# Gating of five batches: sums and products on GpSimd, spread over more turns, two batches overlapping

## The chip, the core and the metric

The kernel runs on one core of a Trainium2 chip, with TensorE (PE), VectorE (DVE), ScalarE (ACT), GpSimd (POOL) and the sync engine's DMA queue (SP). The metric is device time in microseconds, median of three executions. One more execution was profiled, and every row below comes from it.

## What is computed

Block-causal attention feeds a mixture-of-experts layer in which every token goes to one expert and every expert keeps at most `capacity` tokens. Cut from the reference:

```
scores = scale * q @ k.T                       # 8 batches x 8 heads, 576 x 64, f32
attn   = softmax(where(block_i >= block_j, scores, -1e9))
x      = (attn @ v) as [B*S, H*D]              # 4608 x 512
logits = x @ w_gate                            # 8 experts
expert_idx = argmax(logits);  gate_w = softmax(logits)[expert_idx]
for e: tok = the `capacity` tokens of e with the largest gate_w
       out[tok] = gate_w[tok] * (relu(x[tok] @ w1[e]) @ w2[e])
```

## The kernel before

The order of every engine's instructions is written out by hand. The main loop has 32 **turns**, one for each pair of heads, four pairs to a batch. The list `TURN` names the steps of a turn and to which pair each belongs: loads five pairs ahead (`load`), preparation of q and k two pairs ahead (`prep`), scores, row maxima (`max`, `merge`) and exponentials (`soft`) of the next pair, and transposes back (`back`), copies out of PSUM (`take`) and products with v (`values`) of the present pair.

Some names that the steps need:

- `merge` (line 593) is one small DVE operation in each turn; ACT's next exponentials read its result. Turns are measured here from one merge to the next, and turn i ends at the merge of pair i+1.
- `prep 0` comes right behind `merge` on DVE (`STREAM_TRANSPOSE`, line 529); GpSimd then scales its result (`qt`, line 536), and the step `ends` (line 570) on PE reads that at the next turn's start. Behind the scaling, GpSimd issues the loads of v (line 522), some of the loads of weights (line 332), and two loads of k (line 514).
- `ends`, `scores 2` (PE, lines 570, 553, then the mask, 579), then `back` (634), `scores 1` and `scores 3`, the mask again, then `values` (652). `max 56 0` is the first DVE maximum of a turn and reads `scores 2`.
- SP issues loads of q and k for the pair five ahead, and the stores of a batch's sums and rows (`store`, lines 387 to 393).

**Gating** of a batch is done in the four turns after its last pair. A queue `small` of generators is advanced by the steps `t`, one instruction each: one `t` opens the turn, `pe` follows it, then come five more, and a seventh stands between `scores 3` and `max 08 1`, shortly before `values`. `pe` issues the logits' products on PE in the first of the four turns and their transposes (`logits2`, line 417) in the second, into the PSUM banks that `scores 1` and `back B` also use.

Per batch the queue holds `recip` (six DVE instructions), `store`, `products` (four DVE products with `rs` into `prod`, line 423, and the sum over heads into `lg`, line 427), `shift` (maximum `mx`, line 432, and difference `dl`), then `expo` on ACT (step `ta`), `first_of` (four DVE instructions), `weight` (three), `turn` (one product on GpSimd into `sp`, line 463), `turn2` (16 small PE matmuls at the head of `values`, line 472) and `placed` (one DVE copy, line 478). Before, these fall as follows:

```
first turn   placed of the batch before, recip 1 to 5; recip 6 in the seventh slot;  PE: logits
second turn  store; products (4), sum over heads; mx in the seventh slot;            PE: logits2
third turn   dl, eq, eq * iota, min, eq;  expo
fourth turn  sum, reciprocal, Gm;  GpSimd: sp;                                       PE: turn2
```

The first of the batches has no `placed` ahead of its `recip`, so that in its first turn (turn 5) all six stand in the opening slots, and no `turn2` was in the turn before. Batch b has its four turns at i = 4b+5 to 4b+8.

Of the kernel before, what the change touches and what calls it, by code (L numbers as in the profile page):

```python
# [7 lines left out]
F32 = mybir.dt.float32  # L8
# [5 lines left out]
ALU = mybir.AluOpType  # L14
AX = mybir.AxisListType
# [3 lines left out]
P = 128  # L19
BLK = 64  # L20
NT = 5
# [148 lines left out]
def tile_attn_moe(ctx, tc, q, k, v, w_gate, w1, w2, capacity, out, xs=None, dbg=None):  # L170
    nc = tc.nc
    B, H, S, D = q.shape
    NTOK, DM = out.shape
    E, _, F = w1.shape
# [18 lines left out]
    sm = att2.enter_context(tc.tile_pool(name="sm", bufs=4))  # L193
# [51 lines left out]
    iota_e = sm1.tile([P, E], F32, name="iota_e")  # L245
    iota_v = sm1.tile([P, NT, E], F32, name="iota_v")
    Gm = const.tile([P, NC, E], F32, name="Gm")
    prod = sm1.tile([P, NT, H, E], F32, name="prod")
# [22 lines left out]
    dl = sm1.tile([P, NT, E + 1], F32, name="dl")  # L271
# [47 lines left out]
    def weights(n, after=None):  # L319
        for _ in loads(n, after):  # L320
            pass

    def loads(n, after=None):

        nonlocal nw, loaded
        for _ in range(n):
            src, e = wlist[nw]
            w_ = wpools[nw % len(wpools)].tile([P, KP * F], F32, name="w")
            nw += 1
            wt_[src is w2, e] = w_ = w_.rearrange("p (a f) -> p a f", f=src.shape[2])  # L330
            if nw <= FW0:
                yield from (nc.gpsimd.dma_start(w_[:, a], src[e][a * P:(a + 1) * P]) for a in range(w_.shape[1]))
                continue
            with ExitStack() as order:
                if loaded is not None:
                    order.enter_context(tc.issue_after(loaded.ins))
                load = loaded = nc.sync.dma_start(w_, src[e].rearrange("(a p) f -> p a f", p=P))
            if after is not None:
                tc.add_manual_dep(load.ins, after.name, mybir.DependencyInfo(
                    mybir.DependencyClass.Sync, mybir.DependencyReason.DATA))  # L340
# [14 lines left out]
    def banks(use, where=BANKS):  # L355
        return [psp[i].tile([P, 512], F32, name=f"bank{i}") for i in where[use]]

    class Batch:
# [61 lines left out]
        def products(self):  # L420
            for pr in range(NP):
                iv = self.la[pr // 2][:, 0:BLK * NT].rearrange("p (t r c) -> p t r c", t=NT, r=2)[:, :, pr % 2, 0:2 * E]
                yield nc.vector.tensor_tensor(
                    prod[:, :, 2 * pr:2 * pr + 2], iv.rearrange("p t (s e) -> p t s e", s=2),
                    self.rs[:, :, 2 * pr:2 * pr + 2].unsqueeze(3).broadcast_to([P, NT, 2, E]), op=ALU.mult)
            self.lg = sm.tile([P, NT, E], F32, name="lg", bufs=2)
            yield nc.vector.tensor_reduce(self.lg, prod.rearrange("p t h e -> p t e h"), axis=AX.X, op=ALU.add)

# [20 lines left out]
        def weight(self):  # L449
            vec = nc.vector  # L450
            N = NT
            g = sm.tile([P, N], F32, name="g", bufs=2)
            yield vec.tensor_reduce(g, dl, axis=AX.X, op=ALU.add)
            yield vec.reciprocal(g, g)
            yield vec.tensor_tensor(Gm[:, N * self.b:N * (self.b + 1)], self.eq,
                                    g.unsqueeze(2).broadcast_to([P, N, E]), op=ALU.mult)

        def turn(self, eng, n=1):

            self.sp = sp = sm.tile([P, E, NT, 8], F32, name="sp", bufs=1)  # L460
            G = Gm[:, NT * self.b:NT * (self.b + 1)].rearrange("p t e -> p e t")
            for s_ in range(n):
                eng.tensor_tensor(
                    sp[:, s_:E:n], G[:, s_:E:n].unsqueeze(3).broadcast_to([P, E // n, NT, 8]),
                    sameE.unsqueeze(1).unsqueeze(1).broadcast_to([P, E // n, NT, 8]), op=ALU.mult)
# [21 lines left out]
    HW = NW // 2  # L487

    batches = {}

    class Pair:

# [179 lines left out]
    def warm(n, wt, after=None):  # L672

        if not n:
            return
        with ExitStack() as order:
            if after is not None:
                order.enter_context(tc.issue_after(after.ins))
            for i in range(n):
                nc.tensor.matmul(wt.rearrange("p (a c) -> p a c", c=P), lhsT=identr,  # L680
                                 rhs=identr.unsqueeze(1).broadcast_to([P, 4, P]), start=(i == 0), stop=(i == n - 1))

    n = B * NP
# [7 lines left out]
    wg_v = w_gate.rearrange("(r s d) e -> s d r e", s=2, d=D)  # L691
    cleared, kept = 0, 2

    pe_, small, acts, turns, issued = [], [], [], [], {None}

    def enqueue(bt):

        def mark(tag):
            return lambda: issued.add((bt, tag))

        def fill(f, need=None, then=()):
            small.append((f(), need and (bt, need), then))

        pe_.extend(([bt.logits], [bt.logits2, mark("l2")]))
        fill(bt.recip, None, (bt.store,))
        fill(bt.products, "l2")
        fill(bt.shift, None, (mark("sub"),))
        fill(bt.first_of)
        fill(bt.weight, "ge", (lambda: bt.turn(nc.gpsimd), lambda: turns.append((bt, mark("t2")))))
        fill(bt.placed, "t2")  # L710
        acts.append((bt.expo, (bt, "sub"), mark("ge")))

    def pe():
# [1 line left out]
            f()  # L715

    def t():
        while small:
            g_, need, then = small[0]
            if need not in issued or next(g_, None) is not None:  # L720
                return
            small.pop(0)
            for f in then:
                f()

    def ta():
        if acts and acts[0][1] in issued:
# [10 lines left out]
    with tc.manual_schedule():  # L738
        warm(WARM[0], banks("g")[0])
        early = loads(FW0)  # L740
        for i in range(-LEAD, n):
            if i == -1:
                nc.sync.dma_start(ci, capacity.bitcast(U32).partition_broadcast(P))
                for h in range(2):
                    nc.sync.dma_start(wgd[h * D:(h + 1) * D, :, h * E:(h + 1) * E], wg_v[h])

            for _ in range(min(4, nz - kept - cleared) if i >= n - 5 else 0):
                clear(cleared, nc.sync)
                cleared += 1
            if i == 1 - LEAD:  # L750
                nc.scalar.activation(early_exp, ramp[:, 2, 0:1], AF.Exp)
                constants()
            if i == -1:
                constants2()
            if i == 1:
                constants3()
            if i >= 2 and i % 3:
                next(early, None)
            for d, what, *args in FIRST if i == -1 else AHEAD if i == -2 else TURN if i < n - 1 else LAST:
                if what in slots_:  # L760
                    slots_[what]()
                elif 0 <= i + d < n and not (what == "flip" and n - NP <= i + d < n - 2):
                    getattr(pairs[i + d], what)(*args)
            if n - NP <= i + valued < n - 2:
                pairs[i + valued].flip()
            if i >= flipped and (i - flipped) % NP == NP - 1 and i - flipped < n - 1:
                enqueue(batches[(i - flipped) // NP])
        for _ in early:
            pass
        while not turns:  # L770
            t()
        bt = batches[B - 1]
        pairs[n - 2].flip()
        for _ in bt.recip():
            pass
        bt.store_sums()
        to, from_ = pairs[n - 1].out.pop("V0")
        pairs[n - 1].take("V1", "v")
        nc.scalar.copy(to[:, 0], from_[:, 0])
        nc.vector.tensor_copy(to[:, 1], from_[:, 1])  # L780
        att.close()
        fwa = late.enter_context(tc.tile_pool(name="fwa", bufs=FWA, **right, **tw))
        wpools += [fwa] * FWA
        lt = bt.logits_of()
        pairs[n - 1].flip()
        bt.store_x()
        weights(1)
        bt.logits_out(lt)
        bt.logits2()
        bt_, mark = turns.pop(0)  # L790
        bt_.turn2(banks("av")[0])
        mark()
        for _ in (*bt.products(), *bt.shift()):
            pass
        bt.expo()
        while small:
            t()
        found, weighed = bt.first_of(), bt.weight()
        for g_ in (found, found, found, weighed, found, weighed, weighed):
            next(g_)  # L800
        bt.turn(nc.vector, 2)
        bt.turn2(banks("L")[0])
        for _ in bt.placed():
            pass
# [7 lines left out]
    vec = nc.vector  # L812
    pool = nc.gpsimd
# [323 lines left out]
    with tc.If(again > 0):  # L1137
# [8 lines left out]
        eq = gen.tile([P, CP, E], F32, name="eq")  # L1146
# [15 lines left out]
        step = 1.0  # L1162
# [161 lines left out]
```

## Time and profile before

| | |
|---|---|
| median of 3 executions | 396.84 us (396.63 to 399.62) |
| profiled execution | 397.45 us, span 395.7 us, so 1.75 us lie around the span |
| granted TensorE clock | 0.995 of full speed |
| busy share of the span | PE 95%, DVE 72%, ACT 73%, POOL 43% |

The main loop ends at about 280 us; the experts' layer follows. Busy time of PE is modelled from pipelined matmuls, so that a full PE does not say that it is at its peak.

### The profile page before, as it was taken

What the parts mean: (1) busy time and instruction counts of PE and PEld (TensorE: products, weight loads), DVE (VectorE), ACT (ScalarE), POOL (GpSimd) and SP (SyncE); (2) the same over time, 40 slices, a digit from 0 to 9 for tenths busy, and PEclk for the clock granted to TensorE, in tenths of its full rate; (3) what the DMA queues carried; (4) which work ended last, traced back from release to release, by engine and by line L of the source; (5) the groups of instructions that cost most, each with busy time, mean ns of one, the idle gap of its engine ahead of it and who ended that gap; (6) DMA issues with size and microseconds to landing.
All of it is one profiled execution on the core that took longest, in us unless ns stands there. A gap on an engine that the chain in (4) does not pass through costs nothing. (4 is left out here: it accounts for less than half of the span.)

```text
span 395.7 us, 15123 instructions
## 1 busy us (share of the span) xinstructions
PE 374.4 (95%) x5963; PEld 254.8 (64%) x5963; DVE 285.3 (72%) x812; ACT 290.7 (73%) x886; POOL 171.9 (43%) x333
## 2 busy tenths in 40 slices
PE   5899999999999999999999999998899899999991
PEld 3566766766766766766667667666578745666551
DVE  5879899999999998999999999999764220100000
ACT  1799999999999999999999999999122122333231
POOL 6246664575665567556467544510147010000010
PEclk9999999999999999999999999999999999999997
DMA  9979999899999999999999998999477999999801
GB/s 125 151 125 189 137 183 180 167 214 111 186 170 241 161 136 235 156 156 214 129 153 213 176 151 170 374 383 272 104 244 226 355 398 397 393 398 395 306 22 36
DMA packets 169917, 84.40 MB, mean 213 GB/s; under 512 B 132573, under 2 KB 151869, under 8 KB 169840
## 3 DMA queue, kind: packets, MB, share of 16 engines
q1 hardware_dynamic: 158352, 61.80, 72.5%
q0 software_dynamic: 9120, 21.27, 23.4%
q8 instruction: 49, 0.80, 1.0%
q10 hardware_dynamic: 2368, 0.30, 0.6%
q14 instruction: 28, 0.23, 0.3%
HBM read 63.21 MB, written 20.33 MB: 211 GB/s over the span
## 5 line engine op out<-in xcount | busy, mean ns | idle before, releaser
L600 ACT ACTIVATE P<-bank,negm 128x512 f32<-128x512 f32 (+3 forms) x320 | 158.7, 583 | 11.1 <-DVE negm L589 6.2
L553 PE MATMUL bank<-T,qt 64*128 64x320 f32 (+3 forms) x512 | 98.7, 495 | 1.0 <-DVE PT L670 0.8
L589 DVE TENSOR_REDUCE negm<-bank 128x1 f32<-128x320 f32 (+2 forms) x192 | 83.7, 475 | 8.5 <-PE bank L579 8.4
L652 PE MATMUL bank<-PT,vn 128*64 128x64 f32 (+3 forms) x1280 | 88.1, 293 | 0.6 <-ACT PT L670 0.6
L670 ACT COPY PT<-bank 128x512 f32<-128x512 f32 x158 | 82.6, 669 | 3.6 <-PE bank L634 3.2
L536 POOL TENSOR_SCALAR qt<-T 128x128 f32<-128x128 f32 (+2 forms) x96 | 31.1, 341 | 106.6 <-DVE T L529 106.6
L652 PEld LDWEIGHTS bank<-PT,vn 128*64 128x64 f32 x1280 | 56.3, 137 | 27.1 <-ACT PT L670 4.1
L600 ACT ACTIVATION_READ_ACCUMULATOR P<-bank,negm 128x1 f32 x256 | 70.8, 276 | 0.0
L634 PEld LDWEIGHTS bank<-ident,P 64*128 64x128 f32 (+1 forms) x1600 | 58.9, 137 | 11.9 <-issue 6.3
L634 PE MATMUL bank<-ident,P 64*128 64x64 f32 (+1 forms) x1600 | 64.7, 226 | 1.1 <-ACT P L600 0.6
L553 PEld LDWEIGHTS bank<-T,qt 64*128 64x128 f32 x512 | 46.8, 187 | 27.8 <-ACT PT L670 14.5
L589 DVE TENSOR_REDUCE raw<-bank 128x1 f32<-128x64 f32 (+1 forms) x128 | 52.5, 445 | 2.4 <-PE bank L553 1.6
L529 DVE STREAM_TRANSPOSE T<-ld 128x576 f32<-128x576 f32 x64 | 49.6, 774 | 3.0 <-DMA ld<-in_q_dram 1.7
L522 POOL DMA_DIRECT2D vn<-in_v_dram x58 | 46.0, 799 | 1.6 <-PE bank L658 1.1
L1100 DVE SCALAR_TENSOR_TENSOR y<-av,comb,yt 80x512 f32<-80x512 f32 (+1 forms) x8 | 5.6, 696 | 51.5 <-ACT yt L1099 50.7
L1043 PE MATMUL ps<-xsT,w 128*64 128x80 f32 x1024 | 38.7, 234 | 2.4 <-issue 1.8
L1043 PEld LDWEIGHTS ps<-xsT,w 128*64 128x64 f32 x1024 | 36.6, 137 | 6.0 <-issue 4.7
L1105 POOL DMA_INDIRECT out_dram<-y,si x8 | 7.4, 926 | 74.2 <-DVE y L1100 74.2
L1096 PE MATMUL av<-w,hT 128*32 128x512 f32 (+3 forms) x320 | 39.1, 553 | 0.0
L514 POOL DMA_DIRECT2D ld<-in_k_dram x54 | 37.5, 704 | 3.5 <-DMA ld<-in_q_dram 2.9
L1099 ACT ACTIVATE yt<-ps,gfar 32x512 f32<-32x512 f32 (+2 forms) x18 | 11.4, 635 | 26.0 <-PE ps L1096 25.8
L1066 ACT ACTIVATE hT<-ps 128x320 f32<-128x320 f32 x16 | 7.0, 437 | 30.6 <-PE ps L1043 30.6
(177 smaller groups left out, 435.3 us busy)
## 6 DMA issues: line engine op xcount, KB each, us to landing
w<-in_moe_w_dram SPq DMA_DIRECT2D x13, 2048.0 KB, 21.6
xs<-Y SPq DMA_DIRECT2D x32, 288.0 KB, 5.8
out_dram<-zero SPq DMA_DIRECT2D x18, 512.0 KB, 7.6
ld<-in_q_dram SPq DMA_DIRECT2D x126, 72.0 KB, 5.5
vn<-in_v_dram POOLq DMA_DIRECT2D x58, 128.0 KB, 5.4
ld<-in_k_dram SPq DMA_DIRECT2D x72, 72.0 KB, 5.2
w<-in_moe_w_dram POOLq DMA_DIRECT2D x8, 512.0 KB, 7.2
ld<-in_k_dram POOLq DMA_DIRECT2D x54, 72.0 KB, 6.1
```

The lines of the kernel that those rows point to most:

```text
L514: eng.dma_start(self.nat[x][r], (q, k)[x][b, h0 + h, :, 32 * i:32 * i + 32] .rearrange("(g r) d -> r g d", r=32))
L522: eng.dma_start(self.vn[:, h], v[b, h0 + h, 0:512].rearrange("(j p) d -> p j d", p=P))
L529: nc.vector.transpose(t, self.nat[x].rearrange("p g d -> p (g d)"))
L536: nc.gpsimd.tensor_scalar(qb[:, to], tb[:, of], scalar1=SCALE, scalar2=1.0, op0=ALU.mult, op1=ALU.mult)
L553: nc.tensor.matmul(s[h][:, c:c + n], lhsT=q_[:, P * t - BLK:P * t + BLK], rhs=k_[:, 0:n], start=(c == 0 and g != "2"), stop=(g == "1"))
L589: nc.vector.tensor_reduce(to[:, b, h:h + 1], self.s[g][h][:, c:c + n], axis=AX.X, op=ALU.max, negate=True)
L600: nc.scalar.activation(Pt[self.i % 2][u][:, h, c1:c1 + n], self.s[g][h][:, c:c + n], AF.Exp, bias=self.negm[:, t, h:h + 1], scale=1.0, acc ...
L634: nc.tensor.transpose(pt[c][0:cols.stop - cols.start, n_ * BLK:(n_ + 1) * BLK], row[u][r, h, cols], ident[r, r])
L652: nc.tensor.matmul(a4[r] if c0 is None else av[r, BLK * c0:BLK * (c0 + b1 - b0)], lhsT=self.vn[:, h, j, :], rhs=self.PT[:, h, row, b0:b1]. ...
L670: (nc.scalar.copy if (eng or TAKE[x]) == "a" else nc.vector.tensor_copy)(*self.out.pop(x))
L1043: yield nc.tensor.matmul(dst(b)[64 * c:64 * (c + 1)], lhsT=w_[:, a, col:col + 64], rhs=x_[:, a], start=(a == 0), stop=(a == n - 1))
L1096: last = nc.tensor.matmul(to[col:col + s1 - s0, c0:c1], lhsT=hT[:, a, s0:s1], rhs=w_[:, a, c0:c1], start=(a == ends[0]), stop=(a == ends[1 ...
```

## The change

For batches 0 to 4 (`products` returns for them ahead of the sum over heads) the sum over heads, the subtraction, one product, the sum over experts and the product with the gate go from DVE to GpSimd; sums become trees of additions of halves. Every hand-over between DVE and GpSimd waits for the next turn: a generator that yields `HOLD_T` is left alone until then. Each of these batches has a list of its own (`slow`), which gets the slots that `small` leaves, so that a batch's last steps lie beside the first steps of the next. Batches 5, 6 and 7 keep the old steps.

```
+            if self.b < B - 3:
+                return
...
+        def tree(self, src, n, name):
+            while n > 1:
+                n //= 2
...
+                nc.gpsimd.tensor_tensor(to, src[:, :, 0:n], src[:, :, n:2 * n], op=ALU.add)
+                src = to
+            return to
+        def choose(self):
+            lg = self.tree(prod, H, "lg")
...
+            yield HOLD_T
+            yield vec.tensor_reduce(mx, lg, axis=AX.X, op=ALU.max)
...
+            vec.tensor_tensor(eq, lg, mxb, op=ALU.is_equal)
+            pool.tensor_tensor(dl[:, :, 0:E], lg, mxb, op=ALU.subtract)
+            pool.tensor_tensor(eq, eq, iota_e.unsqueeze(1).broadcast_to([P, NT, E]), op=ALU.mult)
+            yield HOLD_T
+        def index(self):
+            yield vec.tensor_reduce(ix, eq, axis=AX.X, op=ALU.min)
+            yield vec.tensor_tensor(eq, iota_v, ix.unsqueeze(2).broadcast_to([P, NT, E]), op=ALU.is_equal)
+        def total(self):
+            g = self.tree(dl, E, "g")
+            nc.gpsimd.tensor_tensor(self.g.unsqueeze(2), g, dl[:, :, E:E + 1], op=ALU.add)
+            yield HOLD_T
+            yield nc.vector.reciprocal(self.g, self.g)
+            yield nc.gpsimd.tensor_tensor(Gm[:, NT * self.b:NT * (self.b + 1)], self.eq,
+                                          self.g.unsqueeze(2).broadcast_to([P, NT, E]), op=ALU.mult)
...
+        if bt.b < B - 3:
+            slow.append([])
+            fill(bt.choose, "pr", (mark("sub"),), slow[-1])
+            fill(bt.index, None, (), slow[-1])
+            fill(bt.total, "ge", turn_, slow[-1])
+            fill(bt.placed, "t2", (), slow[-1])
...
     def t():
+        for of in (small, *slow):
+            while of and not any(of is x for x in held):
+                g_, need, then = of[0]
+                if need not in issued:
+                    break
+                step = next(g_, None)
+                if step is HOLD_T:
+                    held.append(of)
+                if step is not None:
+                    return
...
         for i in range(-LEAD, n):
+            held.clear()
```

## Rows read from the trace of the kernel before

**Rows 1.** DVE in order of time: the merges that end turns 3 to 9.

```profile
44.80 0.21 DVE L593 SCALAR_TENSOR_TENSOR negm<-raw,lower 128x4 f32<-128x4 f32 x1
...
52.63 0.21 DVE L593 SCALAR_TENSOR_TENSOR negm<-raw,lower 128x4 f32<-128x4 f32 x1
...
61.48 0.21 DVE L593 SCALAR_TENSOR_TENSOR negm<-raw,lower 128x4 f32<-128x4 f32 x1
...
70.01 0.22 DVE L593 SCALAR_TENSOR_TENSOR negm<-raw,lower 128x4 f32<-128x4 f32 x1
...
77.77 0.22 DVE L593 SCALAR_TENSOR_TENSOR negm<-raw,lower 128x4 f32<-128x4 f32 x1
...
85.72 0.22 DVE L593 SCALAR_TENSOR_TENSOR negm<-raw,lower 128x4 f32<-128x4 f32 x1
...
94.95 0.22 DVE L593 SCALAR_TENSOR_TENSOR negm<-raw,lower 128x4 f32<-128x4 f32 x1
```

**Rows 2.** Waits, turns 5 to 25: total us, times, longest.

```profile
DVE negm L589 <- PE bank L579: 4.8, 10, 0.7
...
ACT P L600 <- DVE negm L593: 2.0, 10, 0.4
```

**Rows 3.** DVE in order of time, turn 3 (no gating): its first maximum.

```profile
40.60 0.63 DVE L589 TENSOR_REDUCE negm<-bank 128x1 f32<-128x448 f32 x1 [0.75 <-PE bank L579]
```

**Rows 4.** DVE in order of time, turn 14 (second turn of a batch), from prep 0.

```profile
128.54 0.78 DVE L529 STREAM_TRANSPOSE T<-ld 128x576 f32<-128x576 f32 x1
...
131.45 0.69 DVE L423 TENSOR_TENSOR prod<-bank,rs 128x80 f32<-128x80 f32 x4
132.17 0.76 DVE L427 TENSOR_REDUCE lg<-prod 128x40 f32<-128x320 f32 x1
132.83 0.63 DVE L589 TENSOR_REDUCE negm<-bank 128x1 f32<-128x448 f32 x1
...
136.90 0.23 DVE L593 SCALAR_TENSOR_TENSOR negm<-raw,lower 128x4 f32<-128x4 f32 x1
```

**Rows 5.** PE in order of time: turn 3, the end of turn 12, turn 14.

```profile
40.41 1.97 PE L634 MATMUL bank<-ident,P 64*128 64x64 f32 x48
...
44.26 0.93 PE L652 MATMUL bank<-PT,vn 128*64 128x320 f32 x10
...
118.63 0.35 PE L472 MATMUL bank<-sp,sameR 128*32 128x40 f32 x16
118.91 2.75 PE L652 MATMUL bank<-PT,vn 128*64 128x320 f32 x40
...
132.09 1.98 PE L634 MATMUL bank<-ident,P 64*128 64x64 f32 x50
```

**Rows 6.** GpSimd in order of time, end of its loads in turn 14, then turn 15.

```profile
133.16 1.36 POOL L514 DMA_DIRECT2D ld<-in_k_dram  x2
138.00 0.97 POOL L536 TENSOR_SCALAR qt<-T 128x128 f32<-128x128 f32 x3 [3.48 <-DVE T L529]
```

**Rows 7.** GpSimd in order of time: operations with two inputs, and the one behind.

```profile
9.05 0.45 POOL L302 TENSOR_TENSOR before<-before,ident 128x128 f32<-128x128 f32 x1
...
117.54 0.82 POOL L463 TENSOR_TENSOR sp<-Gm,sameE 128x320 f32<-128x320 f32 x1
...
288.59 0.21 POOL L867 TENSOR_TENSOR pen<-pen,iota_c 128x12 f32<-128x12 f32 x1
288.88 0.20 POOL L868 TENSOR_SCALAR pen<-pen 128x6 f32<-128x6 f32 x1
```

**Rows 8.** SP's issues in order of time, turns 11 and 12: q of pair 15, then a store.

```profile
110.73 5.73 SPq L514 DMA_DIRECT2D ld<-in_q_dram  x4
...
117.62 4.91 SPq L393 DMA_DIRECT2D xs<-Y  x4
```

**Rows 9.** DVE and GpSimd in order of time, behind the main loop.

```profile
287.76 0.61 DVE L842 TENSOR_TENSOR spread<-near,sameR 128x192 f32<-128x192 f32 x2
...
287.94 0.24 POOL L859 TENSOR_SCALAR keyn<-key 128x6 f32<-128x6 f32 x1 [0.19 <-DVE key L858]
```

More of the change, by code (lines that the diff above doesn't have):

```diff
@@ L456, in weight @@
                                     g.unsqueeze(2).broadcast_to([P, N, E]), op=ALU.mult)
+        def tree(self, src, n, name):
+            while n > 1:
+                n //= 2
+                shape = list(src.shape)
+                shape[2] = n
+                to = sm.tile(shape, F32, name=f"{name}{n}", bufs=1)
+                nc.gpsimd.tensor_tensor(to, src[:, :, 0:n], src[:, :, n:2 * n], op=ALU.add)
+                src = to
+            return to
+        def choose(self):
+            pool, vec = nc.gpsimd, nc.vector
+            lg = self.tree(prod, H, "lg")
+            lg = lg[:, :, 0]
+            yield HOLD_T
+            mx = sm.tile([P, NT], F32, name="mx", bufs=2)
+            yield vec.tensor_reduce(mx, lg, axis=AX.X, op=ALU.max)
+            mxb = mx.unsqueeze(2).broadcast_to([P, NT, E])
+            self.eq = eq = sm.tile([P, NT, E], F32, name="eq", bufs=2)
+            vec.tensor_tensor(eq, lg, mxb, op=ALU.is_equal)
[3 more added lines that the diff above has]
+        def index(self):
+            vec, eq = nc.vector, self.eq
+            ix = sm.tile([P, NT], F32, name="ix", bufs=2)
+            yield vec.tensor_reduce(ix, eq, axis=AX.X, op=ALU.min)
+            yield vec.tensor_tensor(eq, iota_v, ix.unsqueeze(2).broadcast_to([P, NT, E]), op=ALU.is_equal)
+        def total(self):
+            g = self.tree(dl, E, "g")
+            self.g = sm.tile([P, NT], F32, name="gsum", bufs=2)
+            nc.gpsimd.tensor_tensor(self.g.unsqueeze(2), g, dl[:, :, E:E + 1], op=ALU.add)
[3 more added lines that the diff above has]
+                                          self.g.unsqueeze(2).broadcast_to([P, NT, E]), op=ALU.mult)
         def turn(self, eng, n=1):
@@ L489, in tile_attn_moe @@
     batches = {}
+    HOLD_T = object()
     class Pair:
@@ L692, in tile_attn_moe @@
     cleared, kept = 0, 2
-    pe_, small, acts, turns, issued = [], [], [], [], {None}
+    pe_, small, slow, acts, turns, issued, held = [], [], [], [], [], {None}, []
     def enqueue(bt):
@@ L699, in mark, with fill @@
             return lambda: issued.add((bt, tag))
-        def fill(f, need=None, then=()):
-            small.append((f(), need and (bt, need), then))
+        def fill(f, need=None, then=(), to=small):
+            to.append((f(), need and (bt, need), then))
         pe_.extend(([bt.logits], [bt.logits2, mark("l2")]))
+        turn_ = (lambda: bt.turn(nc.gpsimd), lambda: turns.append((bt, mark("t2"))))
         fill(bt.recip, None, (bt.store,))
[L706 to L710, printed above, removed]
+        fill(bt.products, "l2", (mark("pr"),))
+        if bt.b < B - 3:
[4 more added lines that the diff above has]
+            fill(bt.placed, "t2", (), slow[-1])
+        else:
+            fill(bt.shift, None, (mark("sub"),))
+            fill(bt.first_of)
+            fill(bt.weight, "ge", turn_)
+            fill(bt.placed, "t2")
         acts.append((bt.expo, (bt, "sub"), mark("ge")))
@@ L717, in t @@
     def t():
[L718 to L724, printed above, removed]
+        for of in (small, *slow):
[8 more added lines that the diff above has]
+                    return
+                of.pop(0)
+                for f in then:
+                    f()
     def ta():
```

## Prediction

> **What bounds the kernel now.** I read four views, in this order. The busy shares by slice of the span come first: in the main loop PE, DVE and ACT are all nearly full, so that none of them can be called the bound from its share. So second, DVE in order of time, to get the length of each turn from merge to merge [rows 1]. Turns are 7.83 us long without gating (44.80 to 52.63). With gating they take 8.85 in turn 5, then 8.53, 7.76 and 7.95 for the second, third and fourth turn of batch 0, and 9.23 for turn 9, the first turn of batch 1. The merges of the 21 turns behind repeat these lengths within 0.03, apart from turns 18 and 22 (8.78 and 8.68). So gating costs 33.47 - 4 * 7.83 = 2.15 us a batch, and nearly all of that lies in the first and second turn.
>
> Third, the waits: they say who is late in which turn [rows 2]. In ten of the turns DVE waits for the mask of `scores 2`, so there DVE's own gating costs nothing; these are the first and fourth turns. In ten ACT waits for the merge; these are first and second turns. Fourth, PE and DVE of single turns side by side.
>
> A plain turn shows the pace: DVE stands idle 0.75 us until `scores 2` is there [rows 3], and from this first maximum to the merge it takes 44.80 - 40.60 = 4.20 us. PE sets the pace there: `back` begins at 40.41 and `values` 3.85 later, at 44.26 [rows 5], which is 0.54 ahead of the merge.
>
> In a second turn it is DVE: its four products end at 132.14, the sum over heads follows at 132.17, and the first maximum begins only at 132.83 [rows 4], though PE was already at `back` at 132.09 [rows 5]. In the plain turn the maximum followed `back`'s start by 0.19, so here it is 132.83 - 132.28 = 0.55 late.
>
> **First turns** (9, 13, 17, 21, 25). `placed` leaves the opening slots, the reciprocal moves up into them, and `turn2` no longer precedes. Turn 5 of the old kernel is just this turn, and took 8.85 against 9.23 [rows 1]: 0.38 less. The 16 small products of `turn2` push `values` from 118.63 to 118.91 [rows 5], 0.28 of it; the rest is the reciprocal. Against that `expo` moves to the turn before and can delay ACT there by up to the 0.12 by which the old fourth turn exceeds a plain one [rows 1]; I take half of it. So 0.32 * 5 = 1.6 us gained, 1.3 at the low end and 1.9 at the high. The new GpSimd tree of four small sums lies in GpSimd's idle time (3.48 in the turn of [rows 6]; four times 0.21 [rows 7]).
>
> **Second turns** (6, 10, 14, 18, 22). The sum over heads and `mx` leave DVE. The maximum then starts at 132.28, and with 4.20 of a plain turn the merge falls at 136.48 instead of 136.90 [rows 4]: 0.42 less. The rest of the 0.55 and the 0.18 of `mx` aren't gained, because `scores 1`, behind PE's late `back`, is next late. The reciprocal that is added to the opening slots lies before the products, whose transposes on PE come no earlier; it costs nothing while it ends before 131.45. Gain 0.42 * 5 = 2.1 us (1.5 to 2.7).
>
> **Third turns.** Before, DVE did its five instructions and the turn took 7.76, so taking them away gives nothing. But `turn2` now stands at the end of the second turn: `values` would start at 132.09 + 3.85 + 0.28 = 136.22, that is 0.26 ahead of the new merge instead of 0.54, and PE sets the pace of the third turn by that 0.28. I count 0.3 lost in turns 11, 15, 19 and 23 and 0.07 in turn 7 (7.76 to the plain 7.83): 1.3 us lost. Slack could hide this: nothing lost is one bound, 0.35 * 5 = 1.75 the other. `placed`, `mx` and `eq` in the opening slots are covered by the 0.75 idle of DVE.
>
> **Fourth turns** (8, 12, 16, 20, 24): 7.95 becomes the plain 7.83, since `expo` no longer runs ahead of it and `turn2` is gone; 0.6 us gained (0.3 to 0.6). The two DVE instructions that are left hide behind the same idle time.
>
> **Batch 5 and SP.** Turn 27 gets batch 4's `turn2` besides batch 5's in turn 28: 0.28 of PE's time, I take 0.25 lost (0 to 0.3). On SP a batch's store is moved: it is issued in the seventh slot of the first turn instead of the first slot of the second, and so passes the loads of that second turn. SP is behind its program here: q of pair 15, whose last issue ends at 116.46 and which lands some 5 us later by the DMA issues' medians, is read at 128.54 [rows 4, 8], a margin of 7. The store holds SP for about 6 (116.5 to 122.5) [rows 8], and turns that are 2 us shorter by then take the rest. I count 0.3 lost in turn 13 (0 to 1). Later loads have more room.
>
> **GpSimd.** Ten small operations a batch are new to it. Its prices: 0.82 for 320 elements, 0.45 for 128, 0.21 for 12 [rows 7], so between them about 0.51 for 160, 0.35 for 80 and 0.27 for 40, and 0.08 from the end of one to the start of the next that needs it. The tightest place is the second turn. Its loads end at 134.52 [rows 6]; `Gm` is there at 134.79, `sp` at 135.68, while PE asks for it at 132.09 + 3.85 = 135.94: 0.26 to spare. The tree over heads, 1.13 and three hand-overs, ends at 137.1, and the scaling of q, which began at 138.00 and will be wanted 0.42 earlier, has 0.45 to spare. Zero cost, then, while these prices hold.
>
> **The sum**: 1.6 + 2.1 + 0.6 gained, 1.3 + 0.25 + 0.3 lost, so 2.45 us. The profiled execution would go from 397.45 to 395.0. It was 0.6 above the median, and the gain is taken from the median too: 396.84 - 2.45 = 394.4.
>
> A rule of the Trainium skill stands against the change. The row first: in the second turn GpSimd would be in the tree over heads (135.7 to 137.1) when DVE comes to the merge (136.48), an operation with two inputs in SBUF that ACT waits for. Two DVE products of two SBUF inputs ran beside a GpSimd operation behind the main loop, and GpSimd's took 0.24 where its like took 0.20 to 0.21 [rows 7, 9]; the pair of DVE operations shows no gap. The Trainium skill, "SBUF — State Buffer", section "SBUF: two separate sides", says that GpSimd and a DVE instruction with two SBUF inputs exclude each other for a whole instruction when the GpSimd one reads SBUF. No row here shows that at more than the 0.04 of this one. By the row the sum stays; by the rule up to 0.35 is lost in each of five merges, 1.75, and the time is 396.2.
>
> **Rivals.**
> *The merge waits for GpSimd's tree.* If the tree's addition running at 136.48 must end first, the merge is up to 0.35 late in each of five second turns. Against it stands the row just told, with 0.04; for it, that nothing in the main loop yet puts both there. Together with a third turn at its dearer bound it gives back 1.75 + 0.45, and the time is 396.6. The Trainium skill's page named above would have it so.
> *The third turn does not give it back.* ACT and DVE have slack in the third turn, and `values` there waits for ACT's copies as much as for PE. Then 1.3 is not lost, nor the 0.3 of SP: 4.05 gained, 392.8.
> *GpSimd is late in the second turn* (the slower side). Between the loads' end and the scaling of q there are 137.58 - 134.52 = 3.06 us, plus 0.24 by which the scaling may be late before `ends` on PE feels it; the added work is 0.27 + 0.81 + 1.13 and four hand-overs, 2.5. All prices 1.3 times the rows' fill this; each further tenth costs 0.25 in four second turns. From 1.6 times on the kernel is slower than before; at 1.8 times the loss is 1.2 * 4 = 4.8, and the time 399.2. The rows' prices are for flat operands, and those of the tree are halves of a strided tile: that speaks for it. The 320 elements of `sp`, also strided, at 2.6 ns each speak against it.
>
> **How the numbers follow.** The forecast, 394.4, has a chance of 0.58; the merge behind the tree 0.18; the third turn free 0.15; GpSimd late 0.09. One per cent, 3.97 us, is about what a measurement can tell from no change. The range goes from the third turn free to just past the merge rival, 392.6 to 397.0; beyond it lies GpSimd late and part of the others' edges. Faster by over 1% is below 392.9: half of the free third turn and a little of the forecast's upper edge, 0.12. Slower by over 1%, above 400.8, needs GpSimd at twice its prices: 0.03. The rest, 0.85, is within.
>
> **What would show it.** Merges 8.85 to 8.98 apart in first turns, 8.1 in second, 8.1 in third, 7.83 in fourth turns; DVE's first maximum of the second turn right behind the products with an idle gap for PE; `turn2` on PE with no wait for `sp`; the scaling of q still released by DVE's transpose and not by GpSimd's own queue. A longer merge in second turns says that the ports exclude each other; `ends` waiting for `qt` says that GpSimd is late; DVE's transpose waiting for a load in turn 13 says that the store's new place matters. The prediction is wrong if third turns stay at 7.8, or if turns that I left alone grow.

## The result, and the profile after

| | before | after |
|---|---|---|
| median of 20 executions each | 397.66 us (396.63 to 399.62) | 393.17 us (391.95 to 399.44) |
| profiled execution | 397.45 us, span 395.7 | 393.76 us, span 392.0 |
| granted TensorE clock | 0.995 | 0.992 |

The ratio is 0.9895, 95% interval 0.9874 to 0.9916: 4.5 us faster by the medians, 3.7 by the two profiled executions, where 2.45 was forecast. Here and below, medians and ranges are of all executions, and ratios leave out those more than 1.5% above the fastest of the same kernel. The first part of the page shows the moved work: DVE had 285.3 us in 812 instructions and GpSimd 171.9 in 333; PE's count is unchanged.

```profile
PE 372.4 (95%) x5963; PEld 252.9 (65%) x5963; DVE 279.8 (71%) x787; ACT 290.0 (74%) x886; POOL 185.4 (47%) x383
```

DVE after, in order of time: the merges that end turns 3 to 14 (start, duration), to be laid beside [rows 1].

```profile
44.94 0.21 DVE L637 SCALAR_TENSOR_TENSOR negm<-raw,lower 128x4 f32<-128x4 f32 x1
...
52.78 0.21 DVE L637 SCALAR_TENSOR_TENSOR negm<-raw,lower 128x4 f32<-128x4 f32 x1
...
61.64 0.21 DVE L637 SCALAR_TENSOR_TENSOR negm<-raw,lower 128x4 f32<-128x4 f32 x1
...
69.75 0.21 DVE L637 SCALAR_TENSOR_TENSOR negm<-raw,lower 128x4 f32<-128x4 f32 x1
...
77.51 0.21 DVE L637 SCALAR_TENSOR_TENSOR negm<-raw,lower 128x4 f32<-128x4 f32 x1
...
85.36 0.21 DVE L637 SCALAR_TENSOR_TENSOR negm<-raw,lower 128x4 f32<-128x4 f32 x1
...
94.34 0.21 DVE L637 SCALAR_TENSOR_TENSOR negm<-raw,lower 128x4 f32<-128x4 f32 x1
...
102.38 0.21 DVE L637 SCALAR_TENSOR_TENSOR negm<-raw,lower 128x4 f32<-128x4 f32 x1
...
110.22 0.21 DVE L637 SCALAR_TENSOR_TENSOR negm<-raw,lower 128x4 f32<-128x4 f32 x1
...
118.00 0.21 DVE L637 SCALAR_TENSOR_TENSOR negm<-raw,lower 128x4 f32<-128x4 f32 x1
...
126.97 0.21 DVE L637 SCALAR_TENSOR_TENSOR negm<-raw,lower 128x4 f32<-128x4 f32 x1
...
135.01 0.21 DVE L637 SCALAR_TENSOR_TENSOR negm<-raw,lower 128x4 f32<-128x4 f32 x1
```

Their differences, with those of the later batches, by turn of the batch and against the forecast ("gain" is summed over the turns of one kind):

| turn | before | forecast | after | gain forecast | gain measured |
|---|---|---|---|---|---|
| first (9, 13, 17, 21, 25) | 9.23 | 8.85 to 8.98 | 8.98 | 1.6 | 1.28 |
| second (6, 10, 14, 18, 22) | 8.49 to 8.78 | 8.1 | 8.04 to 8.28 | 2.1 | 2.46 |
| third (7, 11, 15, 19, 23) | 7.76 | 8.1 | 7.76; 7.83; turn 15 8.28 | -1.3 | -0.70 |
| fourth (8, 12, 16, 20, 24) | 7.95 | 7.83 | 7.85; 7.78 | 0.6 | 0.82 |
| 26 to 30, SP's term | | | | -0.55 | -0.07 |

From the merge that ends turn 4 to that of turn 30 it was 218.54 us and is 214.78. What lies behind the last merge is unchanged: 124.54 and 124.47. So the whole gain is in the turns that the change touches, and the row that differs most from the forecast is the third. Of its 0.70, 0.50 lies in turn 15 alone and does not come back in the second profile of the same kernel (y_again, below), where turn 15 took 7.83; that execution gained 4.43 in the loop.

The waits of turns 6 to 25 (total us, times, longest): against 4.8 us in ten turns [rows 2], DVE now waits for the mask in all 20. ACT waits for a merge once instead of ten times, and GpSimd's scaling of q still waits for DVE's transpose in every turn.

```profile
POOL qt L580 <- DVE T L573: 47.5, 20, 3.8
...
DVE negm L633 <- PE bank L623: 7.0, 20, 0.5
...
ACT P L644 <- DVE negm L637: 0.2, 1, 0.2
```

GpSimd after in turn 14, from its loads of k (where [rows 6] had 3.48 idle) to the scaling of q:

```profile
131.73 1.36 POOL L558 DMA_DIRECT2D ld<-in_k_dram  x2
133.11 0.27 POOL L498 TENSOR_TENSOR Gm<-eq,gsum 128x40 f32<-128x40 f32 x1
133.47 0.79 POOL L506 TENSOR_TENSOR sp<-Gm,sameE 128x320 f32<-128x320 f32 x1
134.22 0.52 POOL L467 TENSOR_TENSOR lg<-prod 128x160 f32<-128x160 f32 x1
134.82 0.71 POOL L467 TENSOR_TENSOR lg<-lg 128x80 f32<-128x80 f32 x2
136.08 0.98 POOL L580 TENSOR_SCALAR qt<-T 128x128 f32<-128x128 f32 x3 [0.55 <-DVE T L573]
```

`Gm` 0.27, `sp` 0.79, the tree 0.52, then 0.36 and 0.27 (the 0.71 of the row at 134.82 holds both, with 0.08 between): the prices forecast were 0.27, 0.81 and 0.51, 0.35, 0.27. 0.55 is left, forecast 0.45.

DVE after in the same turn: the first maximum waits 0.15 for PE, as the forecast wanted to see, 130.88 - 126.97 = 3.91 after the merge, where it was 132.83 - 128.41 = 4.42.

```profile
130.88 0.63 DVE L633 TENSOR_REDUCE negm<-bank 128x1 f32<-128x448 f32 x1 [0.15 <-PE bank L623]
```

PE after: `back` of a plain turn (4) and of a third turn (11), then the end of turn 14.

```profile
48.38 1.97 PE L678 MATMUL bank<-ident,P 64*128 64x64 f32 x48
...
106.04 1.68 PE L678 MATMUL bank<-ident,P 64*128 64x64 f32 x48
...
134.43 0.35 PE L515 MATMUL bank<-sp,sameR 128*32 128x40 f32 x16
134.71 2.75 PE L696 MATMUL bank<-PT,vn 128*64 128x320 f32 x40
```

Here is why the third turn gave nearly nothing back. `turn2` does push `back` of turn 11 to 106.04 - 102.38 = 3.66 behind the merge, where a plain turn has 48.38 - 44.94 = 3.44 and turn 11 before had 3.36. But its 48 transposes take 1.68 instead of 1.97, and are done at the same time after the merge, 5.34 against 5.41 in the plain turn and 5.33 in turn 11 before. A plain `back` holds 0.28 of waiting inside it, which the rows, merged as they are, don't show as idle time. By the trace's semaphores it stops twice: until ACT's last exponential is done, and until ACT has copied the last `values` out of PSUM into `xT`. ACT in order of time, turns 4 and 11:

```profile
48.28 0.64 ACT L644 ACTIVATE P<-bank,negm 128x320 f32<-128x320 f32 x1
...
48.78 0.81 ACT L714 COPY xT<-bank 128x64 f32<-128x64 f32 x2
...
105.72 0.56 ACT L644 ACTIVATE P<-bank,negm 128x320 f32<-128x320 f32 x1
...
106.22 0.74 ACT L714 COPY xT<-bank 128x64 f32<-128x64 f32 x2
```

The exponentials end 48.92 - 48.38 = 0.54 after the plain `back` has begun, and 106.28 - 106.04 = 0.24 after that of turn 11. The copies end 4.65 and 4.58 behind the merge. A `back` that begins 0.2 or 0.3 later runs through without stopping.

The same slack shows on DVE, turn 11:

```profile
106.23 0.62 DVE L633 TENSOR_REDUCE negm<-bank 128x1 f32<-128x448 f32 x1 [0.54 <-PE bank L623]
```

From here to the merge it takes 3.98, without idle time, where a plain turn takes 4.20 with short waits in it. So a third turn now lasts until its first maximum, 3.85 behind the merge, and 3.98 more.

### The profile page after: what moved, and what is told of

It reads as the page before. It is cut to its first block, busy times and chain, and to the rows that moved or that the text cites. A ratio compares the mean times of both kernels' runs of the same rounds, so it can differ in the third digit from the quotient of the medians.

```text
span 392.0 us, 15147 instructions
## 1 busy us (share of the span) xinstructions
PE 372.4 (95%) x5963; PEld 252.9 (65%) x5963; DVE 279.8 (71%) x787; ACT 290.0 (74%) x886; POOL 185.4 (47%) x383
## 5 line engine op out<-in xcount | busy, mean ns | idle before, releaser
L644 ACT ACTIVATION_READ_ACCUMULATOR P<-bank,negm 128x1 f32 x256 | 70.0, 274 | 0.0
L597 PEld LDWEIGHTS bank<-T,qt 64*128 64x128 f32 x512 | 48.1, 188 | 26.5 <-ACT PT L714 15.2
L633 DVE TENSOR_REDUCE raw<-bank 128x1 f32<-128x64 f32 (+1 forms) x128 | 51.7, 443 | 2.8 <-PE bank L597 1.9
L1102 PE MATMUL ps<-xsT,w 128*64 128x80 f32 x1024 | 39.9, 238 | 2.2 <-issue 1.7
L1102 PEld LDWEIGHTS ps<-xsT,w 128*64 128x64 f32 x1024 | 37.8, 140 | 5.8 <-issue 4.5
L1155 PE MATMUL av<-w,hT 128*32 128x512 f32 (+2 forms) x320 | 39.0, 553 | 0.0
```

What stands on the lines that cost most here:

```text
L597: nc.tensor.matmul(s[h][:, c:c + n], lhsT=q_[:, P * t - BLK:P * t + BLK], rhs=k_[:, 0:n], start=(c == 0 and g != "2"), stop=(g == "1"))
L633: nc.vector.tensor_reduce(to[:, b, h:h + 1], self.s[g][h][:, c:c + n], axis=AX.X, op=ALU.max, negate=True)
L644: nc.scalar.activation(Pt[self.i % 2][u][:, h, c1:c1 + n], self.s[g][h][:, c:c + n], AF.Exp, bias=self.negm[:, t, h:h + 1], scale=1.0, acc ...
L1102: yield nc.tensor.matmul(dst(b)[64 * c:64 * (c + 1)], lhsT=w_[:, a, col:col + 64], rhs=x_[:, a], start=(a == 0), stop=(a == n - 1))
L1155: last = nc.tensor.matmul(to[col:col + s1 - s0, c0:c1], lhsT=hT[:, a, s0:s1], rhs=w_[:, a, c0:c1], start=(a == ends[0]), stop=(a == ends[1 ...
```

## Experiments

The two theories: *places* (DVE's second turn was too long, and the gain comes from work that is put where DVE waited for PE anyway, on whichever engine) and *work* (the gain comes from DVE's having less to do). All changes below are made to the kernel after, and all turn lengths are those of the one profiled execution of each kernel. "Loop" is the time from the merge of turn 4 to that of turn 30 that a kernel saves against before; the kernel after saves 3.76, and 4.43 in its second profile.

**x_sum_dve: the sum over heads alone back on DVE, in the slot where the tree is issued.**

```
-            lg = self.tree(prod, H, "lg")
-            lg = lg[:, :, 0]
...
+            lg = sm.tile([P, NT, E], F32, name="lgd", bufs=2)
+            vec.tensor_reduce(lg, prod.rearrange("p t h e -> p t e h"), axis=AX.X, op=ALU.add)
```

> The changed kernel with one thing undone: the sum over heads is again one reduction on VectorE, in the same slot of the second turn; all else stays as changed. Theory of places (a VectorE instruction costs only where the next merge waits for VectorE): second turns go from 8.04 back to 8.5 or 8.6, first, third and fourth turns stay at 8.98, 7.83 and 7.78, so about 2.5 us slower than the changed kernel and still 1.5 us faster than the kernel before. Theory of work (each us of VectorE work counts the same anywhere): 5 * 0.76 = 3.8 us slower than the changed kernel, nothing left of the gain.

396.27 us (before 397.73), ratio 0.9971, interval 0.9939 to 1.0003; loop 1.31: not told from before by the ratio. Second turns are 8.44 (turn 6) and 8.68 to 8.92, longer than the 8.5 or 8.6 expected; first turns are as after, third and fourth at 7.77 and 7.85. DVE in order of time, turn 14: the 0.72 of the sum stands ahead of the merge, which comes 8.68 after the last one (127.67).

```profile
134.79 0.72 DVE L475 TENSOR_REDUCE lgd<-prod 128x40 f32<-128x320 f32 x1
...
136.35 0.21 DVE L637 SCALAR_TENSOR_TENSOR negm<-raw,lower 128x4 f32<-128x4 f32 x1
```

One instruction in five turns carries 2.5 us of the loop, 3.1 against the second profile of the kernel after. It sits behind the seventh slot now and not ahead of the first maximum, so this doesn't yet tell place from engine.

**x_small_dve: the small operations (subtraction, product, sum over experts, `Gm`) on DVE, the sum over heads on GpSimd.**

```
-            pool.tensor_tensor(dl[:, :, 0:E], lg, mxb, op=ALU.subtract)
-            pool.tensor_tensor(eq, eq, iota_e.unsqueeze(1).broadcast_to([P, NT, E]), op=ALU.mult)
...
+            vec.tensor_tensor(dl[:, :, 0:E], lg, mxb, op=ALU.subtract)
+            vec.tensor_tensor(eq, eq, iota_e.unsqueeze(1).broadcast_to([P, NT, E]), op=ALU.mult)
...
-            g = self.tree(dl, E, "g")
...
+            nc.vector.tensor_reduce(self.g, dl, axis=AX.X, op=ALU.add)
...
+            yield nc.vector.tensor_tensor(Gm[:, NT * self.b:NT * (self.b + 1)], self.eq,
```

> The changed kernel with the small operations undone: subtraction, product with the expert numbers, sum over experts and product with the gate are on VectorE again, in the same slots; only the sum over heads stays on GpSimd. Theory of places: third turns unchanged at 7.83 (0.54 us of idle time covers 0.36), first turns 0.1 longer, second turns 0.05 longer: 0.7 us slower than the changed kernel at most. Theory of work: 0.72 us of VectorE work in each of five batches, 3.6 us slower than the changed kernel.

394.92 us, ratio 0.9927 (0.9905 to 0.9949); loop 3.63, 0.13 short of after. First turns are 9.07 (after 8.98), second 8.01, third 7.84 (turn 15 8.23), fourth 7.76. Seven of the ten operations that went to GpSimd in a batch are worth next to nothing there by the turn lengths: DVE hides them where they stand now. The median is 1.8 above that of the kernel after and 1.0 above its second set of runs (y_again), with overlapping intervals of the ratios: more than the 0.7 of the theory of places, less than the 3.6 of the theory of work. The theory of places holds by the turns, and that of work fails.

**x_all_dve: everything but `sp` on DVE, spread over the turns.** As x_small_dve, but with the sum over heads behind the first hold, in the opening slots of the third turn, and the subtraction and the product behind the second, in the fourth.

```
-            lg = self.tree(prod, H, "lg")
-            lg = lg[:, :, 0]
             yield HOLD_T
+            lg = sm.tile([P, NT, E], F32, name="lgd", bufs=2)
+            vec.tensor_reduce(lg, prod.rearrange("p t h e -> p t e h"), axis=AX.X, op=ALU.add)
```

> No gating at all on GpSimd but the old product into sp: everything on VectorE, spread over the turns as in the change, with the sum over heads in the third turn's opening slots and the subtraction and product in the fourth's. Theory of places: third turns 7.83 + 0.2, first 0.1 and second 0.05 longer, so 1.8 us slower than the changed kernel and about 2.4 us faster than the kernel before; the spreading is worth more than half of the gain. Theory of work: no work is taken from VectorE, so the kernel is as slow as before or 7 us slower than the changed one.

396.73 us (393.99 to 401.26), ratio 0.9957 (0.9921 to 0.9993), with a loop of 3.21 in its profiled execution. Third turns are 7.97, first 9.07, one second turn (22) 8.31, in which DVE waited 0.3 for a load of q. DVE in order of time, turn 15: the sum, the maximum and the comparison stand ahead of the first maximum, which begins 138.84 - 134.85 = 3.99 after the merge; in turn 11 of the kernel after it is 3.85. The rest of the turn is 3.98 in both.

```profile
137.75 0.71 DVE L476 TENSOR_REDUCE lgd<-prod 128x40 f32<-128x320 f32 x1
...
138.84 0.62 DVE L632 TENSOR_REDUCE negm<-bank 128x1 f32<-128x448 f32 x1
```

The loop says that places carry most of the gain. By the ratio the gain is 1.7 us, where 2.4 was expected, and the executions lie 7 us apart; the pair y_store_later and y_all_dve_store below was run for that.

**x_ta_later: `expo` five exponentials later, in all batches.** It asks whether `expo`, which now comes in the third turn, keeps first turns at 8.98 rather than at turn 5's 8.86.

```
     (1, "soft", "56", 0),
-    (0, "ta"),
     (1, "soft", "56", 1),
...
     (1, "soft", "08", 1),
+    (0, "ta"),
     (2, "prep", 0),
```

> The changed kernel with the exponential of the gating moved on ScalarE from between the first two exponentials of scores to behind the last one of the 08 tile. If the exponential, which now comes at the end of the fourth turn, is what makes first turns 8.98 instead of the 8.85 of turn 5, they become 8.86 and the kernel gains 0.5 to 0.6 us over the changed one. If not, first turns stay at 8.98 and nothing changes, or 0.12 is lost in the turn that now holds it.

395.5 us (393.05 to 396.81), ratio 0.9929 (0.9887 to 0.9971). First turns stay at 8.97 to 8.98: it isn't `expo`. One turn of the profiled execution, 14, took 11.42. DVE in order of time there:

```profile
128.81 0.78 DVE L573 STREAM_TRANSPOSE T<-ld 128x576 f32<-128x576 f32 x1 [2.10 <-issue]
```

The trace names no releaser, but by the DMA records this transpose's q landed only then. TensorE's granted clock was 0.71 from 130 to 134 us and 0.86 from 134 to 138. The other turns are as after; why the median is 2.3 above that of the kernel after stays open, since the other executions have no trace.

**x_turn2_twice: the 16 products of `turn2` twice over in batches 0 to 4** (the same values are written again). One execution each, 401.20 us beside 401.88 of before, so that only the turns can be read.

```
-            for s_ in range(2):
+            for s_ in (0, 1, 0, 1) if self.b < B - 3 else (0, 1):
```

> The changed kernel with the 16 small products of turn2 on TensorE issued twice for batches 0 to 4, 0.28 us more of TensorE's work ahead of the values in second turns. As predicted (TensorE sets the pace from the values on): third turns 0.28 longer, 1.2 to 1.4 us in all. If TensorE has room in third turns because it waits there for ScalarE anyway: third turns stay within 0.1 of 7.83.

Third turns 11, 15 and 23 took 7.97 against 7.83. PE in order of time, `back` of turn 11, then the end of turn 14:

```profile
109.22 1.68 PE L678 MATMUL bank<-ident,P 64*128 64x64 f32 x48
...
137.57 0.49 PE L515 MATMUL bank<-sp,sameR 128*32 128x40 f32 x32
137.99 2.75 PE L696 MATMUL bank<-PT,vn 128*64 128x320 f32 x40
```

`values` begins 0.42 behind the first of the products, where it was 0.28 in the kernel after. So the second set costs PE 0.14 and not the 0.28 expected, and the third turn pays all of it: `back` of turn 11 begins 3.79 behind the merge (105.43) instead of 3.66, still takes 1.68, and the turn is 0.14 longer. The 0.28 of the change itself had cost 0.07. So the slack inside `back` is used up by the change as it is, and work beyond it costs its full time.

Two turns were longer for other reasons. In turn 19, 8.93 long, PE stood 0.72 inside `values`, and the trace names no releaser. Turn 10 took 11.19, for a load of q. DVE in order of time there, then the windows around it (window; busy of PE, PEld, DVE, ACT, GpSimd; granted clock; DMA share; GB/s).

```profile
96.30 0.78 DVE L573 STREAM_TRANSPOSE T<-ld 128x576 f32<-128x576 f32 x1 [1.86 <-DMA ld<-in_q_dram]
```

```profile
97.00:100.00 3.00, 2.04 (x22) 1.15 (x24) 2.79 (x11) 2.16 (x10) 2.75 (x6) 0.85 0.57 93
100.00:103.00 3.00, 3.00 (x56) 2.70 (x54) 2.12 (x5) 1.55 (x4) 2.90 (x6) 0.58 1.11 188
103.00:106.00 3.00, 3.00 (x58) 2.12 (x57) 2.64 (x7) 2.94 (x8) 1.55 (x4) 1.00 1.10 230
```

**x_tree_twice: each addition of the tree over heads issued twice**, 1.3 us more on GpSimd in each second turn. One execution each, 397.83 beside 401.88.

```
-                nc.gpsimd.tensor_tensor(to, src[:, :, 0:n], src[:, :, n:2 * n], op=ALU.add)
+                for _ in range(2 if name == "lg" else 1):
+                    nc.gpsimd.tensor_tensor(to, src[:, :, 0:n], src[:, :, n:2 * n], op=ALU.add)
```

> The changed kernel with every addition of the tree over heads issued twice, 1.1 to 1.4 us more on GpSimd in second turns. By the prediction's margins (0.4 us before the scaling of q is late, 0.24 before TensorE feels it): the scaling starts about 0.9 us late, and TensorE loses 0.5 to 0.7 us at the start of each of five third turns, 2.5 to 3.5 us in all. If there is more room there, third turns stay at 7.83. If the merge waits for GpSimd's additions, merges get longer than 0.22 or come later in the second turn.

Second turns stay at 8.04; it is the third that pays, 8.22 (11, 23) and 8.41 (15), while 7 and 19, in whose second turns GpSimd issues no load of weights, stay at 7.75 and 7.84. In turn 15, 0.2 of this comes behind the first maximum, as in turn 15 of the kernel after. GpSimd in order of time, then the merge on DVE, at the end of turn 10, and what reads the scaled q on PE:

```profile
101.58 1.12 POOL L468 TENSOR_TENSOR lg<-prod 128x160 f32<-128x160 f32 x2
102.79 1.49 POOL L468 TENSOR_TENSOR lg<-lg 128x80 f32<-128x80 f32 x4
104.25 0.97 POOL L581 TENSOR_SCALAR qt<-T 128x128 f32<-128x128 f32 x3
```

```profile
102.39 0.34 DVE L638 SCALAR_TENSOR_TENSOR negm<-raw,lower 128x4 f32<-128x4 f32 x1
```

```profile
104.93 0.68 PE L615 MATMUL bank<-T,qt 64*64 64x64 f32 x8
```

The scaling of q no longer waits for DVE but follows GpSimd's own additions, some 0.8 late. The eight products of `ends`, 0.30 in the kernel after, take 0.68 here, and 0.39 reaches the turn. That is the mechanism of "GpSimd is late", with a price below the 0.5 to 0.7 expected, in three turns and not in five; at the tree as it is it doesn't show.

The merge took 0.34 here, and 0.29 to 0.34 in the second turns 14, 18 and 22 too, where every merge of the kernel after takes 0.21 to 0.22. It ends at 102.73, and the second addition of 160 at 102.70; in all four turns the merge ends 0.02 to 0.03 behind an addition. So a DVE operation with two inputs in SBUF does wait for GpSimd's addition. The Trainium skill, "SBUF — State Buffer", section "SBUF: two separate sides", has them exclude each other; these rows agree with it. In the kernel after it is free: the addition of 0.36 that begins at 134.82 ends at 135.18, and the merge, from 135.01, ends at 135.22 as it would alone.

**x_no_hold: the second hold taken out**, so that the minimum follows GpSimd's product within one turn. One execution each, 417.76 beside 401.88.

```
-            yield HOLD_T
+            yield eq
```

> The changed kernel without the second hold: VectorE's minimum over the experts comes one slot behind the product on GpSimd, in the third turn, instead of a turn later. GpSimd gets to that product only at 6.4 us of the third turn, behind its loads, so VectorE would wait in the opening slots from 3.3 to 6.7 and the third turn would grow by 2.8 us, 14 us in five batches. If the hand-over a turn later is not needed, nothing changes.

Third turns 11, 19 and 23 took 11.02 to 11.06, turn 15 10.88, and 7 12.40; three of the fourth turns, 8, 16 and 20, took 8.62 to 9.09, which wasn't expected. The loop is 20.3 longer than after. Waits of turns 6 to 25 (total, times, longest), then GpSimd and DVE in order of time, turn 11:

```profile
DVE ix L489 <- POOL eq L483: 16.9, 5, 3.9
```

```profile
112.60 1.37 POOL L558 DMA_DIRECT2D ld<-in_k_dram  x2
...
114.03 0.27 POOL L482 TENSOR_TENSOR dl<-lg,mx 128x40 f32<-128x40 f32 x1
114.25 0.28 POOL L483 TENSOR_TENSOR eq<-eq,iota_e 128x40 f32<-128x40 f32 x1
```

```profile
110.98 0.20 DVE L481 TENSOR_TENSOR eq<-lg,mx 128x40 f32<-128x40 f32 x1
114.56 0.20 DVE L489 TENSOR_REDUCE ix<-eq 128x5 f32<-128x40 f32 x1 [3.38 <-POOL eq L483]
```

DVE asks for a product of 0.28 and waits 3.38, since GpSimd's queue has the turn's loads first. This hold is what makes the hand-over from GpSimd free.

**y_again, y_store_later, y_all_dve_store.** Three kernels beside the same runs of before (397.58): the kernel after unchanged; the same with a batch's store of rows put behind the loads of its second turn, where it was for all batches but the first, whose store stood ahead of them in the old kernel too; and that with everything but `sp` on DVE, as in x_all_dve.

```
-        fill(bt.recip, None, (bt.store,))
+        fill(bt.recip, None, (lambda: stores.append(bt.store),) if bt.b <= B - 3 else (bt.store,))
...
     def t():
+        while due:
+            due.pop(0)()
...
             held.clear()
...
+            due.extend(stores)
+            stores.clear()
```

> The changed kernel once more, unchanged, as the measure for the two beside it on the same chip: about 1 per cent faster than before, turn lengths as in its first profile (8.98, 8.04, 7.83, 7.78). By the theory of the loads' lead, q of the pairs that stand behind a store in the sync engine's queue lands within 3 us of its use in turns 9, 13 and 17, and some of the executions lose about 3 us there.

> The changed kernel with one thing put back: a batch's store is issued behind the loads of the second turn again, in its opening slot, instead of ahead of them. Theory of the lead: q in turns 13, 17 and 21 lands 5 us or more ahead of its use again, 7 and 12 us as before; turn lengths stay the same where nothing was late, so the fastest executions are within 0.3 us of the changed kernel's, but the median is 0.5 to 1.5 us lower and the spread smaller. If the store's place does not matter, medians and spread are those of the changed kernel, and what varies between executions is something else.

> All of the gating on VectorE but the product into sp, spread over the turns as in the change, with the store behind the loads again. Theory of places: third turns 7.97, first 9.07, all else as in the changed kernel: 0.2 us a batch, 0.5 to 1 us slower than the kernel beside it with the additions on GpSimd, and 0.7 to 0.9 per cent faster than before. Theory of work taken from VectorE: as slow as before.

| kernel | median us (range) | ratio (95%) | loop |
|---|---|---|---|
| y_again | 393.94 (393.29 to 395.48) | 0.9910 (0.9882 to 0.9938) | 4.43 |
| y_store_later | 394.19 (393.68 to 394.53) | 0.9908 (0.9884 to 0.9931) | 3.64 |
| y_all_dve_store | 395.10 (393.50 to 395.21) | 0.9925 (0.9901 to 0.9950) | 3.27 |

With the store out of the way the kernel with all on DVE keeps about 70% of the gain (3.27 of 4.43 in the loop, and 2.5 of 3.6 by the medians). Its ratio is clear of 1 but not of that of y_again; it is the turns that tell the two apart, third ones of 7.97 against 7.83 and first ones of 9.08 against 8.97. So *places* carries most, and GpSimd's taking over gives about 0.2 us more a batch. Without GpSimd the sum of 0.7 has to stand somewhere on DVE, and the third turn's opening slots hide all but 0.14 of it.

The store's place does what the prediction said of SP, and the median doesn't show it. SP's issues in order of time, y_again and then y_store_later, turns 10 to 12: the store stands ahead of the q loads in the first and behind them in the second.

```profile
108.25 5.21 SPq L393 DMA_DIRECT2D xs<-Y  x4
...
116.36 5.32 SPq L558 DMA_DIRECT2D ld<-in_q_dram  x4
```

```profile
105.05 3.39 SPq L558 DMA_DIRECT2D ld<-in_q_dram  x4
...
112.46 5.60 SPq L393 DMA_DIRECT2D xs<-Y  x4
```

From landing to transpose, q had 1.3, 7.4, 12.7 and 14.5 us to spare in turns 9, 13, 17 and 21 of before (the landings by the DMA records), 0.9, 2.6, 0.5 and 3.0 after, and 16.0, 12.3, 13.3 and 13.9 with the store behind. (The 1.3 belongs to the first batch, whose store was ahead already.) The median is no lower, a miss; the range is 0.85 us against 2.19, of six executions each, too few to tell the spread.

## Why the prediction was right, and where it was off

The direction, the place of the gain and the order of size held: 393.17 lies in the range and 1.2 below 394.4. Before was at 397.66 in these runs rather than at 396.84, so the gain itself was under-forecast, 2.45 against 3.7 to 4.5. That the median came as near as 1.2 is luck in part: taken from 397.66, the same forecast would have been 395.2, 2.0 too high. Term by term:

- **Second turns**, forecast 2.1, measured 2.46: the sum over heads left the stretch ahead of the merge, and the first maximum moved up by 0.51 (turn 14). Of that 0.06 was given back on the way to the merge, where the forecast gave back 0.13. With the sum back on DVE in this turn (x_sum_dve) all of it is gone.
- **First turns**, 1.6 forecast, 1.28 measured. They stopped at 8.98 in place of turn 5's 8.86. `back` there begins 0.12 later than in turn 5 by the trace; `expo` is not the cause, and what is stays open.
- **Third turns**: this is the step that failed. The prediction gave as a sign of being wrong that third turns stay at 7.8, and they do. "PE sets the pace of the third turn by that 0.28" took `back`'s start for PE's pace, and a full PE for a PE at work. PE had 0.28 of waits for ACT inside `back`, and the `turn2` that came ahead of it used just that time. The 4.20 of a plain turn, which the forecast took as fixed from the first maximum to the merge, shrank with it to 3.98, and 3.85 + 3.98 is the 7.83 measured. The same 3.98 stands behind a first maximum at 3.99 in x_turn2_twice, at 4.23 in x_tree_twice and at 3.99 in x_all_dve. 0.07 was lost in each of turns 11, 19 and 23 and nothing in turn 7, so 0.2 to 0.3 where 1.3 was forecast. The rival "the third turn does not give it back" is what happened, for the reason that it named, slack in front of `values`; its figure, 392.8, is the nearest of the four to the measured 393.17.
- **Fourth turns**, 0.6 forecast, 0.82 measured: 7.78 in four of five, below a plain 7.83.
- **Batch 5**, 0.25 lost forecast, 0.04 measured in turns 27 and 28, by the same slack: `back` of turn 28 begins 0.13 later than before and ends 0.02 later.
- **SP**, 0.3 forecast in turn 13: nothing in either profiled execution of this kernel, but the margin went from 7.4 to 2.6 us. In x_ta_later, with the store in this place, the margin was used up and one turn lost 3.4. So the term is nothing in one execution and ten times as much in another. That this wait comes of the store's place follows from the margins; the kernel wasn't run with the store behind. The 3.2 lost in turn 10 of x_turn2_twice can't be put down to the moved store: the first batch's store stood ahead of that load before, too, with 1.3 to spare.
- **GpSimd**, forecast at zero by prices from neighbouring sizes: held to 0.02 a step. The 0.2 ahead of `turn2` that the waits put down to `sp` is as long in turn 18, where `sp` had ended 0.97 before, so it isn't a wait for `sp`. Doubling the tree shows how near the edge the scaling of q was.
- **The merge behind the tree** (0.18): the exclusion is real, at most 0.13 us a turn even at twice the tree, and zero in the kernel as it is, where 0.35 was feared.

Turn 15's 0.50 isn't explained. A like excess shows in the traces of x_small_dve and y_store_later (8.23, 8.39) and not in others (7.83, 7.76). In the profiled one, PE stood 0.41 inside `back` and the trace names no releaser. By the DMA records a transfer of 16 KB on the instruction queue (q8) landed 1.72 us before PE went on, 1.59 and 1.55 in those two, and 1.70 before the stop in `values` of x_turn2_twice; in y_again, which doesn't stop, it landed 0.8 us earlier in turn 15. So PE may have waited for its instructions; no run tests that.

## What to carry to other kernels

Before costing work that is put ahead of a stretch on the busiest engine, look at how long the same 48 instructions take in different turns: if they take 1.97 in one and 1.68 in another, the difference may be slack: look for what the instructions wait for. Such slack hides work of its size and no more. Moving work to the turn in which its engine waits anyway gave about 70% of the gain here without another engine; the other engine was worth the rest, and with hand-overs that were given a whole turn; taking out one of them cost 20 us. When a step is moved to the queue of the loads, write down the margin of the load behind it, as well as the mean cost.

## What the runs showed of the hardware

A wait of 1.9 to 2.1 us for a load cost 3.2 to 3.4 us, in two runs. In x_turn2_twice TensorE had work for 2.04 of 3 us in the window with the wait, and was granted 0.85 of its clock there, 0.58 in the next 3 us (between its levels of 1.2 and 2.4 GHz) though it was fully busy by then, and 1.00 in the next. And an operation of 4 elements on DVE took 0.29 to 0.34 in place of 0.21 beside a GpSimd addition, ending 0.02 after it, in four turns out of four.
